# First loads on two queues, a new start order, relu before full-width transposes, and three output tiles side by side, in a fused attention and feed-forward kernel

## The chip, the cores and the metric

The kernel runs on one core of a Trainium2 chip. The metric is the time of one execution on the device in microseconds (us); the kernel before took 325.9 us (median of three runs, 325.85 to 326.36). The granted clock of TensorE was 0.994 to 1.0 of full speed.

## The reference

A linear attention (cosFormer) over 8 batches of 8 heads, 576 positions and head size 64, followed by a gated feed-forward layer over the 4608 tokens:

```python
r   = max(x, 0);  phi(x) = concat(r * cos(theta_s), r * sin(theta_s))   # for q and k, theta_s = pi/2 * s/576
kv  = einsum('bhsf,bhsd->bhfd', phi(k), v)        # 128 x 64 for each head
num = phi(q) @ kv;  den = phi(q) @ sum_s phi(k) + 1e-6
x   = (num / den), heads side by side             # 4608 x 512
g   = x @ w_gate                                  # 512 x 1536
out = (g * sigmoid(g) * (x @ w_val)) @ w_out      # 1536 x 512
```

This is shortened from the reference's code. Per batch and head, `kv` sums phi(k) times v over the positions.

## The kernel before

All matrix work is in bf16. Tokens are handled in nine groups of 512; each group has 12 feed-forward chunks ("chunk 6" is columns 768 to 895 of the gate and value weights) and an output stage of four tiles of 128 tokens. From group two on, a group's attention work is hidden between the products of the group before it. Only at the start is there nothing to hide behind, so the first batch has code of its own. Its inputs are loaded in fp32 by SyncE, in the order in which they are needed; all weights and later inputs are loaded by GpSimd:

```python
load_first("v", slice(0, 2))
load_first("v", slice(2, 4))
load_first("q", slice(0, G), 0, 2)          # q of the first two slots only
load_first("k", slice(0, 2))
load_first("k", slice(2, 4), 0, KCUT)
load_first("k", slice(2, 4), KCUT, NC)
# ... later, GpSimd starts its own loads when a piece of v has landed:
nc.gpsimd.tensor_copy(out=hold, in_=first["v"][:, 1, 0, 0:1])
load_slots(0, "q", QCUT, 4)
# ...
```

ScalarE computes the sines; VectorE then weights v with them, once for each of the four pairs of heads (`vmul`). The order of the first batch's steps on all engines is a list of words. `cq` casts q, `tq` turns (transposes) it, `qr` is its relu, `qw` its weighting, `rk` the relu of k, `kv` the k-v product, `z8` eight products with zeros, put in to keep TensorE busy while it waits, `a` the attention product, `den rec x` the division, `xt xc` the turn of the result, `G V s m` the feed-forward products, silu and multiplication; `@act` and `@dve` choose ScalarE or VectorE:

```python
words = """
    cq0@act cq1@act tq0 qr0@dve qw0.0 qw0.1 rk1.0@act rk0.0@dve z8 kv0.0 rk3.0@dve rk2.0@dve kv1.0
    # ... cut ...
```

q of the second batch is turned by TensorE in the middle of group one (the kernel's group 0). Two transposes of half width, one for each half of a head pair, fill one block of 128 columns; the relu is part of the copy out of the bank:

```python
def qturn_pe(b, j, lo, hi, eng):
    ps = take(1).bitcast(BF16).rearrange("p (c x) -> p c x", x=P)
    for c in range(lo, hi):
        for i in range(2):
            nc.tensor.transpose(out=ps[i * D:(i + 1) * D, c - lo], in_=raws[b, "q"][:, 2 * j + i, c],
                                identity=ident)
    relu_op(eng, qt_of(b)[:, :, j, lo:hi].rearrange("p e c s -> p c e s"), ...)
```

In three places: `turn_last` (four half transposes behind chunk 9), the main turn before the k-v product of batch two (28), and a second turn in the output stage (eight). Chunks 6 to 11 of this group run in two halves of 256 tokens.

## Time and profile before

| What (us from the span's start) | Before |
|---|---|
| Time, median of four runs beside the changed kernel | 325.88 |
| Profiled span | 324.6 |
| TensorE busy | 98% |
| First v lands / first q lands / k's first half lands | 4.4 / 8.0 / 9.5 |
| First k-v product | 11.00 |
| Chunk 6 starts | 28.75 |
| Main turn of batch two's q | 39.66 |
| Group two starts (its first gate product) | 55.48 |

The timeline of the kernel before (columns: start, length, engine, line, operation, shapes, count, and in brackets the idle time before it and what ended that) near its start:

```profile
4.44 1.36 DVE L236 TENSOR_TENSOR v<-wo_sb,tab 128x1152 bf16<-128x1152 f32 x1 [0.41 <-DMA wo_sb<-in_v_dram]
10.29 1.53 DVE L217 TENSOR_SCALAR raw_k<-ht 128x576 bf16<-128x576 f32 x5
11.99 0.74 POOL L203 DMA_DIRECT2D wg_sb<-in_moe_w_gate_dram  x1 [1.40 <-DMA raw_q<-in_q_dram]
```

VectorE waits only 0.41 us for v. Its relus of k fall into a stretch (10.6 to 12.0) in which GpSimd issues nothing. And the timeline of the same kernel in the output stage, around the second turn, with the main turn ahead:

```profile
39.66 0.97 PE L264 MATMUL banks<-ident,raw_q 128*64 128x128 bf16 x28
...
52.22 1.03 PE L539 MATMUL banks<-wo_sb,ht 128*128 128x512 bf16 x4
53.18 0.41 PE L264 MATMUL banks<-ident,raw_q 128*64 128x128 bf16 x8
53.52 1.04 PE L539 MATMUL banks<-wo_sb,ht 128*128 128x512 bf16 x4
```

A length in such a line runs to the modelled end of the last product, so read the distance of starts. Four products of 512 columns take 4 x 0.216 = 0.86 us, but from 52.22 to 53.18 it is 0.96: about 0.1 us passes at the change to half width, and then 0.34 us for the eight transposes.

The landing times come from the DMA issues of the first microseconds (what, queue, count, size, us from issue to landing, the median where there are several); q was issued at 1.75:

```profile
wo_sb<-in_v_dram SPq DMA_DIRECT2D x2, 576.0 KB, 4.1
first_q<-in_q_dram SPq DMA_DIRECT2D x1, 256.0 KB, 6.2
```

(v is loaded into the home of the output weights, hence its name. Its two halves took 3.6 and 4.6 us; issued at 0.74 and 1.27, they landed at about 4.4 and 5.9.)

### The profile page before, as it was taken

What the parts mean: (1) busy time and instruction counts of PE and PEld (TensorE: products, weight loads), DVE (VectorE), ACT (ScalarE), POOL (GpSimd) and SP (SyncE); (2) the same over time, 40 slices, a digit from 0 to 9 for tenths busy, and PEclk for the clock granted to TensorE, in tenths of its full rate; (3) what the DMA queues carried; (4) which work ended last, traced back from release to release, by engine and by line L of the source; (5) the groups of instructions that cost most, each with busy time, mean ns of one, the idle gap of its engine ahead of it and who ended that gap; (6) DMA issues with size and microseconds to landing.
All of it is one profiled execution on the core that took longest, in us unless ns stands there. A gap on an engine that the chain in (4) does not pass through costs nothing.

```text
span 324.6 us, 6212 instructions
## 1 busy us (share of the span) xinstructions
PE 318.0 (98%) x2474; PEld 164.6 (51%) x2474; DVE 181.8 (56%) x366; ACT 132.3 (41%) x247; POOL 34.8 (11%) x58
## 2 busy tenths in 40 slices
PE   7999999999999999999999999999999999999995
PEld 3589855454545444544454445444554445444443
DVE  7775866976575647565657555755564236423420
ACT  7553565943653335332642354344432132213311
POOL 6755200002002000110002000200000000000000
PEclk9999999999999999999999999999999999999999
DMA  7999999499676997699689969794921411240014
GB/s 264 215 199 199 205 205 221 70 125 149 147 125 80 185 153 128 93 170 163 120 111 140 164 129 130 119 186 110 134 46 34 106 26 32 44 103 17 2 32 97
DMA packets 71660, 40.37 MB, mean 124 GB/s; under 512 B 47184, under 2 KB 66384, under 8 KB 71632
## 3 DMA queue, kind: packets, MB, share of 16 engines
q1 hardware_dynamic: 49280, 22.29, 37.9%
q0 software_dynamic: 22192, 17.57, 35.5%
q8 instruction: 19, 0.31, 0.4%
q10 hardware_dynamic: 160, 0.13, 0.1%
q14 instruction: 9, 0.07, 0.1%
HBM read 37.75 MB, written 9.44 MB: 145 GB/s over the span
## 4 chain that ended last, share of the span: by engine, by line
PE 95%; DMA 2%; DVE 1%; ACT 0%; SPq 0%; issue 0%; ACTq 0%
PE banks L503 58%; PE banks L539 28%; PE banks L276 3%; PE banks L390 2%; DMA first_q<-in_q_dram 2%; PE banks L475 1%; PE banks L434 1%; PE banks L149 1%; PE banks L558 1%; PE banks L264 0%; PE banks L316 0%; PE banks L372 0%; SPq L117 0%; DVE qwT L360 0%; ACT ob L561 0%; ACT qf L339 0%
## 5 line engine op out<-in xcount | busy, mean ns | idle before, releaser
L514 DVE TENSOR_TENSOR ht<-sg,banks 128x512 bf16<-128x512 bf16 (+2 forms) x122 | 75.8, 625 | 68.1 <-PE banks L503 62.3
L509 ACT ACTIVATE sg<-banks 128x512 bf16<-128x512 f32 (+2 forms) x122 | 66.9, 548 | 113.6 <-PE banks L503 109.0
L503 PE MATMUL banks<-xT,wv_sb 128*128 128x512 bf16 (+2 forms) x488 | 112.8, 355 | 0.1
L503 PE MATMUL banks<-xT,wg_sb 128*128 128x512 bf16 (+2 forms) x488 | 112.6, 355 | 0.0
L539 PE MATMUL banks<-wo_sb,ht 128*128 128x512 bf16 x420 | 94.3, 379 | 0.0
L503 PEld LDWEIGHTS <-wv_sb 128*128 128x128 bf16 x488 | 47.2, 98 | 46.7 <-issue 0.4
L503 PEld LDWEIGHTS <-wg_sb 128*128 128x128 bf16 x488 | 45.7, 98 | 41.6
L539 PEld LDWEIGHTS <-ht 128*128 128x128 bf16 x420 | 40.1, 98 | 45.2 <-issue 0.2
L546 ACT COPY ob<-banks 128x512 f32<-128x512 f32 x18 | 10.5, 585 | 51.2 <-PE banks L539 49.2
L232 DVE TENSOR_TENSOR r_q<-raw_q,tab 128x1152 bf16<-128x1152 bf16 x24 | 17.9, 754 | 20.2 <-ACT raw_q L215 20.2
L546 DVE COPY ob<-banks 128x512 f32<-128x512 f32 x17 | 11.8, 691 | 28.9 <-PE banks L539 28.0
L236 DVE TENSOR_TENSOR v<-raw_v,tab 128x1152 bf16<-128x1152 bf16 x31 | 23.0, 752 | 0.3 <-ACT raw_v L570 0.3
L411 DVE TENSOR_TENSOR x<-banks,rec 128x512 bf16<-128x512 f32 (+1 forms) x32 | 21.5, 674 | 1.1
L714 POOL COPY hold<-phit 1x2 bf16<-1x2 bf16 x5 | 0.9, 176 | 155.1 <-DMA phit<-r_q 155.1
L215 ACT ACTIVATE raw_q<-raw_q 128x576 bf16<-128x576 bf16 x24 | 15.7, 680 | 0.8 <-DMA raw_q<-in_q_dram 0.8
L215 ACT ACTIVATE raw_k<-raw_k 128x576 bf16<-128x576 bf16 x24 | 16.0, 675 | 0.0
L390 PEld LDWEIGHTS <-phit 128*128 128x128 bf16 (+1 forms) x240 | 9.9, 100 | 6.0 <-issue 1.3
L390 PE MATMUL banks<-kv,phit 128*128 128x65 bf16 (+1 forms) x240 | 11.5, 195 | 0.0
L149 PE MATMUL banks<-zeros 128*128 128x64 bf16 (+1 forms) x66 | 8.7, 290 | 1.0 <-DVE zeros L144 1.0
L299 DVE CAST kv<-banks 64x260 bf16<-64x260 f32 x12 | 5.1, 428 | 7.4 <-ACT kv L299 7.4
L276 PEld LDWEIGHTS <-raw_k 64*64 64x64 bf16 x504 | 7.5, 106 | 2.6 <-issue 2.1
L276 PE MATMUL banks<-v,raw_k 64*64 64x130 bf16 x504 | 8.7, 218 | 0.0
(79 smaller groups left out, 134.3 us busy)
## 6 DMA issues: line engine op xcount, KB each, us to landing
out_dram<-ob SPq DMA_DIRECT2D x70, 128.0 KB, 2.4
raw_k<-in_k_dram POOLq DMA_DIRECT2D x7, 576.0 KB, 9.6
raw_q<-in_q_dram POOLq DMA_DIRECT2D x6, 576.0 KB, 6.1
raw_v<-in_v_dram POOLq DMA_DIRECT2D x6, 576.0 KB, 12.3
wo_sb<-in_moe_w_out_dram POOLq DMA_DIRECT2D x3, 512.0 KB, 12.7
wg_sb<-in_moe_w_gate_dram POOLq DMA_DIRECT2D x5, 256.0 KB, 9.0
wv_sb<-in_moe_w_val_dram POOLq DMA_DIRECT2D x5, 256.0 KB, 9.2
wo_sb<-in_v_dram SPq DMA_DIRECT2D x2, 576.0 KB, 4.1
```

The costliest lines, as they stand in the source:

```text
L149: nc.tensor.matmul(out=ps, lhsT=zeros, rhs=zeros[:, 0:cols].unsqueeze(1).to_broadcast([P, 4, cols]), start=True, stop=True)
L215: nc.scalar.activation(out=out, in_=in_, func=AF.Relu)
L232: nc.vector.tensor_tensor(out=st[b, "q"][:, g], in0=o.unsqueeze(2).to_broadcast([P, NC, 2, D]), in1=tab, op=ALU.mult)
L236: nc.vector.tensor_tensor(out=v2s[b % 2][:, g, :, :, 0:D], in0=(first if b == 0 and g == 0 else {"v": raw_of(b, "v")})["v"][:, g].unsqueez ...
L276: nc.tensor.matmul(out=ps[i * D:(i + 1) * D, e, j * 2 * D1:(j + 1) * 2 * D1], lhsT=raws[b, "k"][es, g, c], rhs=v2s[b % 2][es, g, c, :, 0:D ...
L390: nc.tensor.matmul(out=ps[ms, e, g * D1:(g + 1) * D1], lhsT=phit[b][:, e, g, c:c + n].rearrange("p c s -> p (c s)"), rhs=kv2s[b % 2][:, e, ...
L411: nc.vector.tensor_tensor(out=st["x", t].rearrange("p (y e d) -> p e y d", e=2, d=D)[:, :, ys], in0=ps[:, :, 0:2 * J * D1].rearrange("p e ...
L503: nc.tensor.matmul(out=st["f", tg, fc, lo][i], lhsT=(wg_sb, wv_sb)[i][:, kc, fs], rhs=xT[tg][:, ts, kc], start=(kc == 0), stop=(kc == KC - 1))
L509: nc.scalar.activation(out=sg[:, 0:n], in_=st["f", tg, fc, lo][0], func=AF.Silu)
L514: nc.vector.tensor_tensor(out=hts[tg % 2][:, fc, r:r + n], in0=st.pop(("s", tg, fc, lo))[:, 0:n], in1=ps[1], op=ALU.mult)
L539: nc.tensor.matmul(out=o_ps[t], lhsT=hts[tg % 2][:, fc, r:r + P], rhs=wo_sb[:, fc], start=(fc == 0), stop=(fc == FC - 1))
L546: (nc.scalar.copy if t % 2 == 0 else nc.vector.tensor_copy)(out=ob, in_=ps)
```

## The change

The intent is to shorten the start by issuing the first loads from two engines, to rearrange the start's words for the new landing times, and to save TensorE's small costs in group one. The diff, cut to its core:

```diff
     load_first("v", slice(0, 2))
-    load_first("v", slice(2, 4))
+    load_first("v", slice(2, 4), queue=nc.scalar)
     load_first("q", slice(0, G), 0, 2)
-    load_first("k", slice(0, 2))
+    load_first("k", slice(0, 2), queue=nc.scalar)
     load_first("k", slice(2, 4), 0, KCUT)
-    load_first("k", slice(2, 4), KCUT, NC)
+    load_first("k", slice(2, 4), KCUT, NC, queue=nc.scalar)
 # ... qturn_pe: from the relued copy, full width
-            for i in range(2):
-                nc.tensor.transpose(out=ps[i * D:(i + 1) * D, c - lo], in_=raws[b, "q"][:, 2 * j + i, c],
-                                    identity=ident)
-        relu_op(eng, ...)
+            nc.tensor.transpose(out=ps[:, c - lo], in_=st["qp"][:, b, c, j], identity=ident)
+        copy_op(eng, ...)
 # ... words: the whole list is new; its beginning
-        cq0@act cq1@act tq0 qr0@dve qw0.0 qw0.1 rk1.0@act rk0.0@dve z8 kv0.0 rk3.0@dve rk2.0@dve kv1.0
+        cq1@act cq0@dve tq0 qr0@dve rk0.0@act rk1.0@dve qw0.0 qw0.1 z6 kv0.0 rk2.0@dve rk3.0@dve kv1.0
 # ... batch two's v weightings (vmul) and the new relu between them, on VectorE
-    for g, s in enumerate(("a10", "a11", "b8", "b9")):
+    for g, s in enumerate(("b9", "b9", "b10", "b10")):
         at(s, lambda g=g: vmul(1, g))
+        if g == 2:
+            at(s, lambda: relu_slots(1, 0, CUT))
 # ... chunks 6 to 11 in one piece; three output tiles side by side
-    for nm, f in order:
-        ffn_fc(0, f, *((HALF, GH) if nm == "b" else (0, HALF)))
-        slot(f"{nm}{f}")
+    for f in range(6, FC):
+        ffn_fc(0, f)
+        slot(f"a{f}")
+        slot(f"b{f}")
-    steps0 = [(piece, t) for piece in range(3) for t in range(2)] + [(piece, t) for t in (2, 3) for piece in range(3)]
+    steps0 = [(piece, t) for piece in range(3) for t in range(3)] + [(piece, 3) for piece in range(3)]
```

Cut: the choice of a PSUM bank, pool sizes, the division in two halves, small relus at other slots, and the move of one relu of batch two's k from VectorE to ScalarE.

More of the change, by code (lines that the diff above doesn't have):

```diff
@@ L50 @@
     phip = ctx.enter_context(tc.tile_pool(name="phip", bufs=2))
-    xp = ctx.enter_context(tc.tile_pool(name="xp", bufs=3))
+    xp = ctx.enter_context(tc.tile_pool(name="xp", bufs=4))
     xtp = ctx.enter_context(tc.tile_pool(name="xtp", bufs=3))
     smp = ctx.enter_context(tc.tile_pool(name="smp", bufs=3))
-    sgp = ctx.enter_context(tc.tile_pool(name="sgp", bufs=4))
+    sgp = ctx.enter_context(tc.tile_pool(name="sgp", bufs=5))
     obp = ctx.enter_context(tc.tile_pool(name="obp", bufs=4))
@@ L66, in take @@
     def take(n, hold=None):
-        free = [b for b in range(0, 8, n) if not any(b <= x < b + n for r in held.values() for x in r)]
-        b0 = min(free, key=lambda b: sorted(used[b:b + n], reverse=True))
+        taken = {x for r in held.values() for x in r}
+        free = [b for b in range(0, 8, n) if not any(b <= x < b + n for x in taken)]
+        b0 = min(free, key=lambda b: (n == 1 and hold is not None and hold[0] == "o" and b ^ 1 not in taken,
+                                      sorted(used[b:b + n], reverse=True)))
         if hold is not None:
@@ L114, with load_first @@
         first[nm] = flat.bitcast(FP32).rearrange("p (g c d) -> p g c d", g=G, c=NC)
-    def load_first(nm, gs, lo=0, hi=NC):
-        nc.sync.dma_start(out=first[nm][:, gs, lo:hi].rearrange("p g c d -> p g (c d)"),
+    def load_first(nm, gs, lo=0, hi=NC, queue=nc.sync):
+        queue.dma_start(out=first[nm][:, gs, lo:hi].rearrange("p g c d -> p g (c d)"),
                           in_=source(0, nm)[:, gs, lo * D:hi * D])
@@ L258, in qturn_dma, with relu_slots @@
         )
+    def relu_slots(b, lo, hi):
+        if "qp" not in st:
+            both = rel.tile([P, G, NC, 2, D], BF16, name="r_q").rearrange("p g c w d -> p (g c w d)")
+            st["qp"] = both.rearrange("p (b c j x) -> p b c j x", b=2, c=NC, j=J)
+        relu_op("dve", st["qp"][:, b, lo:hi].rearrange("p c j (i d) -> p c (j i) d", i=2),
+                raws[b, "q"][:, :, lo:hi].rearrange("p g c d -> p c g d"))
     def qturn_pe(b, j, lo, hi, eng):
@@ L262, in qturn_pe @@
         for c in range(lo, hi):
-            for i in range(2):
-                nc.tensor.transpose(out=ps[i * D:(i + 1) * D, c - lo], in_=raws[b, "q"][:, 2 * j + i, c],
-                                    identity=ident)
-        relu_op(eng, qt_of(b)[:, :, j, lo:hi].rearrange("p e c s -> p c e s"),
+            nc.tensor.transpose(out=ps[:, c - lo], in_=st["qp"][:, b, c, j], identity=ident)
+        copy_op(eng, qt_of(b)[:, :, j, lo:hi].rearrange("p e c s -> p c e s"),
                 ps[:, 0:hi - lo].rearrange("p c (e s) -> p c e s", e=2))
@@ L395, in a_tile2, with x_den, x_rec @@
         x_of(t, ps)
-    def x_den(t, ps):
-        den = smp.tile([P, H, 1], FP32, name="den")
+    def x_den(t, ps, ys=slice(0, 4)):
+        if ys.start == 0:
+            st["den", t] = smp.tile([P, H, 1], FP32, name="den")
         nc.vector.tensor_single_scalar(
-            out=den.rearrange("p (e y) o -> p e y o", e=2),
-            in_=ps[:, :, 0:2 * J * D1].rearrange("p e (y x) -> p e y x", x=D1)[:, :, :, D:D1], scalar=1e-6, op=ALU.add)
-        st["den", t] = den
-    def x_rec(t):
-        rec = smp.tile([P, H, 1], FP32, name="rec")
-        nc.vector.reciprocal(out=rec, in_=st.pop(("den", t)))
-        st["rec", t] = rec
-        st["x", t] = xp.tile([P, d_model], BF16, name="x")
+            out=st["den", t].rearrange("p (e y) o -> p e y o", e=2)[:, :, ys],
+            in_=ps[:, :, 0:2 * J * D1].rearrange("p e (y x) -> p e y x", x=D1)[:, :, ys, D:D1], scalar=1e-6, op=ALU.add)
+    def x_rec(t, ps, ys=slice(0, 4)):
+        if ys.start == 0:
+            st["rec", t] = smp.tile([P, H, 1], FP32, name="rec")
+            st["x", t] = xp.tile([P, d_model], BF16, name="x")
+        nc.vector.reciprocal(out=st["rec", t].rearrange("p (e y) o -> p e y o", e=2)[:, :, ys],
+                             in_=st["den", t].rearrange("p (e y) o -> p e y o", e=2)[:, :, ys])
     def x_mul(t, ps, ys=slice(0, 4)):
@@ L418, in x_of @@
         x_den(t, ps)
-        x_rec(t)
+        x_rec(t, ps)
         x_mul(t, ps)
@@ L620 @@
     words = """
-        cq0@act cq1@act tq0 qr0@dve qw0.0 qw0.1 rk1.0@act rk0.0@dve z8 kv0.0 rk3.0@dve rk2.0@dve kv1.0
-        kvo00@act rk3.1@dve kvo01@act rk2.1@dve kv1.1 tq1 kvo10@act kvo11@dve a0.0 qr1@dve a0.1 qw1.0 tq3
-        qw1.1 tq2 den0 qr3@act rec0 x0.0 a1.0 a1.1 qr2@act x0.1 xt0.0 qw3.1 xt0.1 xc0.0@act qw3.0 xc0.1@act
-        den1 z2 a3.0 rec1 G1.0 x1.0 a3.1 s1.0 G0.0 V0.0 qw2.0 s0.0 xt1.0 qw2.1 V1.0 xc1.0@dve a2.0 a2.1 m1.0
-        G1.1 den3 den2 V1.1 rec3 s1.1 G2.01 x3.0 G3.01 s2.01 m1.1 V2.01 rec2 s3.01 x2.0 xt3.0 V3.01
-        xc3.0@act m2.01 xt2.0 m3.01 G5.01 xc2.0@dve G4.01 s5.01 m0.0 G0.23 s4.01 V0.23 s0.23 G1.23 m0.23
-        G5.23 s1.23 V1.23 s5.23 V4.01 m1.23 V5.23 m4.01 V5.01 m5.23 G2.23 m5.01 V2.23 s2.23 G3.23 m2.23
-        V3.23 s3.23 G4.23 m3.23 V4.23 s4.23 G0.1 m4.23 V0.1 s0.1 m0.1
+        cq1@act cq0@dve tq0 qr0@dve rk0.0@act rk1.0@dve qw0.0 qw0.1 z6 kv0.0 rk2.0@dve rk3.0@dve kv1.0
+        kvo01@act rk3.1@dve kvo00@act rk2.1@dve kv1.1 a0.0 kvo11@act kvo10@dve tq1 den0.0 rec0.0 a0.1 x0.0
+        qr1@act tq2 den0.1 rec0.1 qw1.1 tq3 qr2@act qw1.0 xt0.0 x0.1 a1.0 qr3@act a1.1 qw2.0 xt0.1 qw2.1
+        xc0.0@act den1 z2 a2.0 rec1 xc0.1@act a2.1 x1.0 G1.0 G0.0 qw3.1 s1.0 xt1.0 s0.0 qw3.0 V0.0 xc1.0@act
+        V1.0 den2 rec2 a3.0 x2.0 a3.1 G0.1 G1.1 den3 s0.1 V1.1 rec3 s1.1 xt2.0 x3.0 G2.01 xc2.0@act V0.1
+        m1.0 V2.01 s2.01 m0.0 m0.1 xt3.0 m1.1 G3.01 m2.01 xc3.0@act V3.01 s3.01 G1.23 m3.01 V1.23 s1.23
+        G0.23 m1.23 V0.23 s0.23 G5.23 m0.23 G4.01 s5.23 G2.23 s4.01 G4.23 s2.23 G5.01 s4.23 V5.01 s5.01
+        V5.23 m5.01 G3.23 m5.23 V3.23 s3.23 V4.23 m3.23 V2.23 m4.23 V4.01 m2.23 m4.01
     """.split()
@@ L634 @@
         whole, a, part = b not in ("0", "1") or a != "0", int(a), int(b or 0)
+        ys = slice(0, 4) if whole else slice(2 * part, 2 * part + 2)
         if op == "z":
@@ L653 @@
         elif op == "den":
-            x_den(a, st["a", a])
+            x_den(a, st["a", a], ys)
         elif op == "rec":
-            x_rec(a)
+            x_rec(a, st["a", a], ys)
         elif op == "x":
-            x_mul(a, st["a", a], slice(0, 4) if whole else slice(2 * part, 2 * part + 2))
+            x_mul(a, st["a", a], ys)
             st["a", a, "n"] = st.get(("a", a, "n"), 0) + 1
@@ L674 @@
                 ffn_mul(0, a, *span)
-    order = []
-    for f in range(6, FC, 2):
-        order += [("a", g) for g in (f, f + 1)]
-        order += [("b", g) for g in (f, f + 1)]
     def turn_last():
@@ L684, in turn_last @@
             qturn_pe(0, j, NC - 1, NC, "act")
+    at("a8", lambda: relu_slots(0, NC - 1, NC))
     at("b9", turn_last)
     at("a8", lambda: relu_k(1, 0, 2, "dve"))
-    at("a9", lambda: relu_k(1, 2, 4, "dve"))
-    for g, s in enumerate(("a10", "a11", "b8", "b9")):
+    at("a9", lambda: relu_k(1, 2, 4, "act"))
+    for g, s in enumerate(("b9", "b9", "b10", "b10")):
         at(s, lambda g=g: vmul(1, g))
+        if g == 2:
+            at(s, lambda: relu_slots(1, 0, CUT))
     at("b11", q_(1, 0, 0), q_(1, 1, 0), lambda: kv_mm(1), lambda: kv_out(1))
@@ L699 @@
     at((2, 0), turn(6, True))
+    at((0, 3), lambda: relu_slots(1, CUT, NC))
     at((2, 1), q_(1, 0, 1), q_(1, 1, 1))
     at((2, 2), turn(7, True))
-    HALF = GH // 2
-    for nm, f in order:
-        ffn_fc(0, f, *((HALF, GH) if nm == "b" else (0, HALF)))
-        slot(f"{nm}{f}")
-    steps0 = [(piece, t) for piece in range(3) for t in range(2)] + [(piece, t) for t in (2, 3) for piece in range(3)]
+    for f in range(6, FC):
[3 more added lines that the diff above has]
+    steps0 = [(piece, t) for piece in range(3) for t in range(3)] + [(piece, 3) for piece in range(3)]
     for i, (piece, t) in enumerate(steps0):
```

## The prediction

> **What bounds the kernel now.** I read the page's busy shares and slices first, then the chain that ended last in order of time, then the groups by shape, the start of the timeline, and the landing of each early transfer.
>
> ```profile
> PE 318.0 (98%) x2474; PEld 164.6 (51%) x2474; DVE 181.8 (56%) x366; ACT 132.3 (41%) x247; POOL 34.8 (11%) x58
> PEclk9999999999999999999999999999999999999999
> L503 PE MATMUL banks<-xT,wv_sb 128*128 128x512 bf16 (+2 forms) x488 | 112.8, 355 | 0.1
> L503 PE MATMUL banks<-xT,wg_sb 128*128 128x512 bf16 (+2 forms) x488 | 112.6, 355 | 0.0
> L539 PE MATMUL banks<-wo_sb,ht 128*128 128x512 bf16 x420 | 94.3, 379 | 0.0
> ```
>
> TensorE is at full clock in every slice and has almost no idle time before its feed-forward products: it is the bound. But a busy TensorE also counts products with zeros, so I look at the chain for time in which it does no useful work.
>
> ```profile
> 1.75 6.24 DMA first_q<-in_q_dram
> 8.01 0.72 ACT qf L339 x2
> 8.78 0.34 PE banks L347 x3
> 9.12 1.73 PE banks L149 x8
> ...
> 12.78 0.43 DVE kvd L324
> 13.21 0.34 DVE qr L217
> 13.58 0.76 DVE qwT L360 x2
> 14.34 0.09 DVE den L399
> ...
> 15.78 0.43 PE banks L149 x2
> ...
> 23.94 11.96 PE banks L503 x112
> 35.90 0.23 PE banks L264 x4
> 36.13 3.60 PE banks L503 x32
> 39.73 0.90 PE banks L264 x28
> 40.63 1.17 PE banks L276 x67
> 41.81 0.97 PE banks L539 x4
> ```
>
> The columns are start, length, what. Useful work starts at 8.5 us, when the first q has landed and been cast. Then come 1.73 us of zero products (L149) that wait for k, and a VectorE stretch from 12.78. Counting every useful product at its streaming time (512 columns: 10.36/48 = 0.216 us; 256: 11.96/112 = 0.107; 128 and 130: 0.055) I get about 306 us; the last matmul ends at 319.8, so 13.6 us are bubbles: 8.5 before the first useful product, about 4.1 from there to 24 us, about 1 after. From the start of token group two's up products (55.5 us) the changed program's TensorE instructions are the same as before, so the change is worth exactly what it moves that point.
>
> **What the Trainium skill says.** (1) "DMA: Bandwidth & Descriptors", Issuing engines are not separate DMA queues: transfers from any engine run on the same 16 DMA engines and interleave; a second issuer saves only sequencer time. The trace agrees as far as it can: with one queue the engines are full from about 2.3 us. The DMA view of the first 45 us, in 40 slices:
>
> ```profile
> DMA  0489999999999999999999999999999999999999
> GB/s 0 72 317 410 343 310 380 349 246 200 182 178 183 201 193 195 197 195 205 193 207 210 198 194 190 191 192 202 217 200 203 202 210 210 206 205 207 208 214 187
> ```
>
> (2) "Perfetto Trace Analysis", DMA Instruction - HWDGE: the issuing sequencer is free for its next instruction only when descriptors are generated. The tail of the timeline agrees: a copy queued behind a ScalarE issue starts after it.
>
> ```profile
> 320.26 0.56 ACTq L564 DMA_DIRECT2D out_dram<-ob  x1
> 320.94 0.32 ACT L561 COPY ob<-banks 128x192 f32<-128x192 f32 x1 [0.71 <-PE banks L558]
> ```
>
> (3) "TensorE: Matmul & The Clock Gate", Back-to-back issue gap: the spacing at full clock grows with the columns (262 cycles for 256, 518 for 512). The trace agrees (107 and 216 ns), so splitting a 512-wide product in two costs almost nothing, and joining it gains almost nothing. (4) Same page, Packing small matmuls: products on different parts of the array run together. The trace agrees: 28 half-width transposes took 0.90 us, 32 ns each, where four full ones take 0.22 us, 55 ns each.
>
> **The change part by part.**
>
> *Two queues.* ScalarE now issues three loads before its table load. At 0.5 to 0.56 us each that is some 1.6 us: its table load would start at 2.3 instead of 0.74, and the sine table be done some 1.0 us later (before, it idled 0.58 us waiting for the angles). VectorE's tab, then its four weightings of v, follow the sine; in the trace the latter end at 4.44 + 1.36 and 6.06 + 2.10 = 8.16, so now near 9.2. The cast of half of q stands behind them on VectorE. Against that, k's first half no longer queues behind q. It landed at 2.27 + 7.2 = 9.5 us; at the measured 350 to 400 GB/s, v (1.18 MB) lands by 5.3 and q and that half of k (0.85 MB, less the share of the GpSimd loads) by about 8. So the 1.73 us wait for k disappears, but the wait for q becomes a wait for VectorE. Estimated: q cast by 9.45, turned by 9.85, relu of q and of k 10.9, first k-v product at 11.0, which is when it starts now. The extra landing time of k is thus spent by the later start of ScalarE, if the issues cost what they cost at the tail; if they hide, all of this is 1 us earlier.
>
> *New order of words.* Before, q's second relu and two weightings (0.34 + 0.76) stood between the k-v copy and the first denominator. They move behind it: 1.1 us off the path to the first x half. But the second half of x now stands behind two weightings, and the token tile that is turned first waits for both. Following the order by hand with these durations, the first gate product comes at about 17.2 (before 16.4), with 0.2 us more of useful work already done and some 0.2 us fewer bubbles after. Net: about 0.3 us late under the full ScalarE delay, 0.7 us early without it.
>
> *Feed-forward chunks 6 to 11 at full width.* Before, twelve half chunks (eight 256-wide products each) took 0.876 us apiece, 10.5 us; 48 products of 0.216 give 10.36. Gain 0.15 us. VectorE and ScalarE save more: twelve evictions of 418 ns become six of 687, off the path.
>
> *Full transposes.* 40 half ones took 0.23 + 0.90 + 0.34 = 1.47 us; 20 full ones at 0.055 take 1.1. Gain 0.37 us. But the relu now comes before the turn, on VectorE, and not in the copy after it. With X the start of chunk 6: VectorE does the chunk-9 product until X + 7.7, two v weightings (1.5), the chunk-10 product (0.69), a third weighting (0.75), then this relu of 1792 elements (estimated 0.7 from 0.45 to 0.65 us for 1152): X + 11.4. TensorE is through with chunk 11 at X + 10.5. It would wait 0.9 us, unless VectorE runs ahead of this count.
>
> *Three output tiles side by side.* Same products. Output weights are needed one to two steps later, which makes room to start earlier (the first third lands near 40.3 and is used at 41.7). No gain by itself.
>
> Sum at the 55.5 us point: +0.3 (or -0.7) -0.15 -0.37 +0.9 (or about 0.3 if the VectorE queue is less full than I count) = +0.7 in the worst reading, -0.9 in the best. The middle is -0.1. The new order has plainly been fitted to the new landing times, so that I lean to the better half and take -0.5: 325.4 us.
>
> **The rivals.** (a) *The start is moved later by ScalarE.* The tail's 0.56 us speaks for it, and the idle 0.58 us before the sine hides only a part. It makes 326 to 326.8. (b) *The weights become the bound.* If the start is 2 us earlier, TensorE meets transfers: chunk 1's value weights land at 8.33 + 7.7 = 16.0 us, batch two's q at 27.16 + 10.6 = 37.8, and through relu (0.7), turns (0.8) and k-v product (1.2) this allows output products no earlier than 40.5, against 41.7 now. So about 1.3 us is the most that the start can give, whatever it does: 324.2 with the rest. Against it: it matters only if all before goes well. (c) *q lands later* because its 512-byte pieces share each DMA engine with k's 2304-byte ones. It took 2.6 us after v for 256 KB even alone on its queue. If it lands at 9.3, the result is that of (a). (d) *PSUM:* three open output tiles leave four banks for the second batch's products; a bank waiting for VectorE's combination (about 1 us for each half) would add 0.2 to 0.5 us.
>
> **Range and chances.** The best case is bounded by the transfers (about -1.5 us), the worst is (a) with the stall at the relu and (d) (about +1.2 us). Low 324.0, high 326.8, centre 325.4. Two percent is 6.5 us, which is more than all bubbles after 8.5 us, and nothing here adds as much: faster by over 2% 0.01, within 2% 0.98, slower by over 2% 0.01.
>
> **What would show it.** Right: k's first half lands over 1 us earlier, no run of six or eight zero products waits for k, ScalarE's sine near 3.6 us, VectorE's weightings of v ending near 9.2, first k-v product near 11.0; a gap of 0.5 to 0.9 us on TensorE before the full transposes, ended by VectorE; the rest shifted as one. Wrong: the first k-v product at 10 or earlier (issues on ScalarE cost nothing), or no wait before the transposes; then the time falls toward 324. Idle TensorE in front of weight loads ended by a DMA would show rival (b), before the second batch's products ended by VectorE rival (d). A time outside the range needs a stall that repeats in each later group, which the unchanged order of instructions there speaks against.

## The result, and the profile after

The changed kernel took 327.95 us (median of four runs, 327.2 to 329.06) against 325.88 (325.66 to 326.36) for the kernel before on the same chip: ratio 1.0063, 95% interval 1.004 to 1.0087. That is within 2%, but slower, and above the predicted range. All outputs are right. A ratio here is always the mean time of one kernel's runs over the mean of the other's in the same rounds, so not quite the ratio of the medians.

The profile's page still says that TensorE is the bound:

```profile
PE 317.8 (97%) x2404; PEld 160.4 (49%) x2404; DVE 182.3 (56%) x362; ACT 133.4 (41%) x244; POOL 34.8 (11%) x58
```

The span went from 324.6 to 326.3. Group two starts at 57.22 instead of 55.48, 1.74 us later, and the last TensorE work ends at 321.52 instead of 319.78, again 1.74. So everything was lost before group two. The chain of the changed kernel (start, length, what):

```profile
1.27 8.10 DMA first_q<-in_q_dram
9.39 0.63 DVE qf L348
...
10.51 0.42 DVE qr L220
10.93 0.73 DVE raw_k L220
...
12.32 1.41 DVE raw_k L220 x4
...
40.59 1.00 DVE r_q L220
41.64 0.96 PE banks L274 x14
```

Before, the chain went through q's landing at 7.99 and was on TensorE from 23.94 on. Now q lands at 9.37, VectorE stands in the chain with its cast and its relus of k, and it comes back at 40.59 with the new relu. The DMA issues of the first microseconds show why the start is late; SyncE issued q at 1.27:

```profile
wo_sb<-in_v_dram SPq DMA_DIRECT2D x1, 576.0 KB, 5.1
wo_sb<-in_v_dram ACTq DMA_DIRECT2D x1, 576.0 KB, 5.5
first_q<-in_q_dram SPq DMA_DIRECT2D x1, 256.0 KB, 8.1
```

q is issued 0.48 us earlier than before and takes 1.9 us longer. The two halves of v no longer land one after the other (4.4 and 5.9) but almost together (5.8 and 6.2): the first half, all that the first weighting needs, now takes 5.1 us instead of 3.6. The timeline lines that answer to those shown of before:

```profile
2.36 1.28 ACT L177 ACT_TABLE_LOAD   x1 [2.36 <-issue]
5.96 1.36 DVE L239 TENSOR_TENSOR v<-wo_sb,tab 128x1152 bf16<-128x1152 f32 x1 [0.88 <-DMA wo_sb<-in_v_dram]
12.25 1.48 DVE L220 TENSOR_SCALAR raw_k<-ht 128x320 bf16<-128x320 f32 x4
12.05 0.82 POOL L206 DMA_DIRECT2D wg_sb<-in_moe_w_gate_dram  x1
...
41.64 0.96 PE L274 MATMUL banks<-ident,r_q 128*128 128x128 bf16 x14 [0.89 <-DVE r_q L220]
```

ScalarE's three issues delay its table load from 0.74 to 2.36. The first v weighting moved from 4.44 to 5.96, still waiting for the load. The main turn waits 0.89 us for VectorE. And in the output stage full transposes fit without a seam:

```profile
54.18 1.03 PE L549 MATMUL banks<-wo_sb,ht 128*128 128x512 bf16 x4
55.05 0.39 PE L274 MATMUL banks<-ident,r_q 128*128 128x128 bf16 x4
55.27 1.03 PE L549 MATMUL banks<-wo_sb,ht 128*128 128x512 bf16 x4
```

0.87 and 0.22 us, where the half transposes needed 0.96 and 0.34.

The balance by distances of starts, in the two traces:

| Step | Before | After | Difference |
|---|---|---|---|
| Chunk 6 starts | 28.75 | 30.12 | +1.37 |
| Chunks 6 to 11 and `turn_last`, to the end of the last product | 10.82 | 10.48 | -0.34 |
| From there to the main turn | 0.09 | 1.04 | +0.95 |
| Main turn, k-v product | 2.08 | 2.06 | -0.02 |
| Output stage | 13.74 | 13.52 | -0.22 |
| Sum: start of group two | 55.48 | 57.22 | +1.74 |

(The last product before the turn starts, as one of four, in a row at 39.13 before and 39.73 after; adding four times 0.109 or 0.216 gives 39.57 and 40.60. The profile's 0.89 us counts from the modelled end of that product, which is 0.15 later. The changed kernel's trace is of an execution of 328.08 us, 0.9 above its fastest, and that of the kernel before of one of 326.36, the slowest of its four. So 1.74 is the difference of these two executions; the medians differ by 2.07 here and by 1.28 in the repetition e5.)

### The profile page after: what moved, and what is told of

It reads as the page before. It is cut to its first block, busy times and chain, and to the rows that moved or that the text cites. A ratio compares the mean times of both kernels' runs of the same rounds, so it can differ in the third digit from the quotient of the medians.

```text
span 326.3 us, 6058 instructions
## 1 busy us (share of the span) xinstructions
PE 317.8 (97%) x2404; PEld 160.4 (49%) x2404; DVE 182.3 (56%) x362; ACT 133.4 (41%) x244; POOL 34.8 (11%) x58
## 4 chain that ended last, share of the span: by engine, by line
PE 93%; DVE 3%; DMA 2%; ACT 0%; issue 0%; ACTq 0%; SPq 0%
PE banks L513 56%; PE banks L549 28%; PE banks L285 3%; DMA first_q<-in_q_dram 2%; PE banks L399 2%; PE banks L485 1%; PE banks L444 1%; PE banks L381 1%; DVE raw_k L220 1%; DVE v L239 1%; PE banks L568 1%; DVE ht L524 0%; DVE qwT L369 0%; PE banks L274 0%; DVE r_q L220 0%; ACT ob L571 0%
## 5 line engine op out<-in xcount | busy, mean ns | idle before, releaser
L524 DVE TENSOR_TENSOR ht<-sg,banks 128x512 bf16<-128x512 bf16 (+2 forms) x116 | 74.8, 650 | 69.3 <-PE banks L513 63.8
L519 ACT ACTIVATE sg<-banks 128x512 bf16<-128x512 f32 (+2 forms) x116 | 65.8, 568 | 111.9 <-PE banks L513 108.1
L513 PE MATMUL banks<-xT,wv_sb 128*128 128x512 bf16 (+2 forms) x464 | 111.3, 364 | 0.0
L513 PE MATMUL banks<-xT,wg_sb 128*128 128x512 bf16 (+2 forms) x464 | 111.2, 364 | 0.0
L513 PEld LDWEIGHTS <-wv_sb 128*128 128x128 bf16 x464 | 44.9, 98 | 48.7
L513 PEld LDWEIGHTS <-wg_sb 128*128 128x128 bf16 x464 | 43.4, 98 | 43.3
L218 ACT ACTIVATE raw_k<-raw_k 128x576 bf16<-128x576 bf16 (+1 forms) x25 | 17.2, 695 | 0.0
```

Of the source, the lines that this page charges most:

```text
L218: nc.scalar.activation(out=out, in_=in_, func=AF.Relu)
L513: nc.tensor.matmul(out=st["f", tg, fc, lo][i], lhsT=(wg_sb, wv_sb)[i][:, kc, fs], rhs=xT[tg][:, ts, kc], start=(kc == 0), stop=(kc == KC - 1))
L519: nc.scalar.activation(out=sg[:, 0:n], in_=st["f", tg, fc, lo][0], func=AF.Silu)
L524: nc.vector.tensor_tensor(out=hts[tg % 2][:, fc, r:r + n], in0=st.pop(("s", tg, fc, lo))[:, 0:n], in1=ps[1], op=ALU.mult)
```

## The experiments

Theory at the outset: the second queue delays the first products, and the relu ahead of the turn adds a stall; the other parts save a little. Rivals: ScalarE's issuing alone is to blame; the new words are; or the runs differ by chance. Twelve kernels were run. All times are us, the first five columns from each kernel's trace, the last two from timed runs.

| Run | q's cast on ScalarE | First k-v product | Chunk 6 | Main turn (wait as the profile counts it) | Group two | Median | Ratio to before, 95% interval |
|---|---|---|---|---|---|---|---|
| before | 8.01 | 11.00 | 28.75 | 39.66 (0) | 55.48 | 325.88 | 1 |
| changed | 9.39 | 11.92 | 30.12 | 41.64 (0.89) | 57.22 | 327.95 | 1.0063, 1.004 to 1.0087 |
| e1 | 7.26 | 10.42 | 28.09 | 39.61 (0.89) | 55.19 | 326.19 | 1.0009, 0.9995 to 1.0023 |
| e2 | 9.09 | 12.26 | 30.24 | 41.15 (0) | 56.97 | 327.86 | 1.0059, 1.0046 to 1.0071 |
| e3 | 9.20 | 11.45 | 29.29 | 40.15 (0.22) | 55.72 | 326.63 | 1.0030, 1.0016 to 1.0045 |
| e4 | 7.94 | 11.00 | 28.75 | 39.66 (0) | 55.48 | 326.16 | 1.0007, 0.9995 to 1.0020 |
| e5 | 9.12 | 11.67 | 29.88 | 41.40 (0.89) | 56.97 | 327.21 | 1.0049, 1.0032 to 1.0065 |
| e6 | 7.75 | 10.53 | 28.21 | 39.00 (0) | 54.94 | 325.64 | 0.9991, 0.9978 to 1.0004 |
| e7 | 7.95 | 11.24 | 29.11 | 40.63 (0.89) | 56.21 | 326.91 | 1.0028, 1.0016 to 1.0040 |
| e8 | 7.51 | 11.34 | 29.28 | 40.80 (0.89) | 56.38 | 327.25 | 1.0040, 1.0028 to 1.0052 |
| e11 | 7.15 | 9.76 | 27.70 | 38.49 (0) | 54.43 | 325.30 | 0.9981, 0.9969 to 0.9993 |
| e12 | 7.58 | 10.57 | 28.31 | 39.10 (0) | 54.92 | 325.82 | 0.9996, 0.9982 to 1.0010 |

(e9 and e10 are not in the table, as they have waits of their own.) A trace is one execution, and the start jitters: with one queue q landed between about 6.9 and 8.0 us, with two between about 9.05 and 9.37, in different runs. A difference of some tenths in one trace proves nothing; I rely on intervals of timed runs, and on traces for where the time is. The medians of "before" in the five sets of rounds were 325.88 to 326.03.

### e1: the changed kernel with all first loads on SyncE

```diff
-    load_first("v", slice(2, 4), queue=nc.scalar)
+    load_first("v", slice(2, 4))
-    load_first("k", slice(0, 2), queue=nc.scalar)
+    load_first("k", slice(0, 2))
-    load_first("k", slice(2, 4), KCUT, NC, queue=nc.scalar)
+    load_first("k", slice(2, 4), KCUT, NC)
```

> The changed kernel with all six first loads back on SyncE, nothing else. Theory (queues are the first cause): q shared each DMA engine with the first half of k and landed at 9.37 instead of 7.99 us, v at 5.9 instead of 4.4; on one queue q lands near 8.0 again, the first k-v product comes near 10.2 (k lands near 9.5) instead of 11.92, and the time falls by 1.3 to 2 us, to about 326.2. Rival (the new word order is what is slow): the start gains under 0.5 us although q lands early.

Measured: 326.19 us, ratio 1.0009; the interval includes 1. Taking the second queue away gives back 1.75 us by the medians with the first runs of the changed kernel (327.95), 1.3 us by ratio with its repetition e5 (1.0049 less 1.0009). The four relus of k are fast again, and GpSimd pauses beside them (from 10.63 to 11.21):

```profile
10.75 0.95 DVE L220 TENSOR_SCALAR raw_k<-ht 128x320 bf16<-128x320 f32 x4
```

The stall before the turn stays at 0.89. So it does not come from the start.

### e2: the kernel before with the loads alternating

```diff
-    load_first("v", slice(2, 4))
+    load_first("v", slice(2, 4), queue=nc.scalar)
-    load_first("k", slice(0, 2))
+    load_first("k", slice(0, 2), queue=nc.scalar)
-    load_first("k", slice(2, 4), KCUT, NC)
+    load_first("k", slice(2, 4), KCUT, NC, queue=nc.scalar)
```

> The kernel before with only the queues alternated. Theory: q lands near 9.4, and because the old order puts both k relus behind q's weightings the start is late by 1 to 1.5 us: 326.9 to 327.4. Rival (queues are harmless, k's earlier landing pays for q's later one): within 0.3 us of 325.9.

Measured: 327.86 us, ratio 1.0059, above the 326.9 to 327.4 expected. Two queues alone, with the old words and the old turns, cost 1.9 us: as much as the whole change. q is cast at 9.09, 1.08 later than before, and TensorE's turn waits for it:

```profile
9.09 0.71 ACT L339 CAST qf<-first_q 128x256 bf16<-128x256 f32 x2 [0.86 <-DMA first_q<-in_q_dram]
```

The five relus of k took 2.34 us together instead of 1.53. Chunk 6 starts 21.15 us after the cast of q here, 20.73 to 20.83 in before, changed, e1 and e5. In these traces, then, the new words take back about 0.4 us of what two queues cost the old ones; in e3's, which has the same start as the changed kernel, it is 1.1 (20.09). With one queue they lie between 0.1 us later (e1) and 0.3 sooner (e6, 20.46). These are single traces.

### e3: the relu of batch two before the third v weighting

```diff
     for g, s in enumerate(("b9", "b9", "b10", "b10")):
-        at(s, lambda g=g: vmul(1, g))
         if g == 2:
             at(s, lambda: relu_slots(1, 0, CUT))
+        at(s, lambda g=g: vmul(1, g))
```

> The changed kernel with the relu of batch two's q put before the third v weighting on VectorE instead of behind it. Theory (the 0.9 us wait of TensorE before the full transposes is VectorE's queue): the wait shrinks by one weighting, 0.7 us, to some 0.2 us, and the time by 0.6 to 0.7 us, to about 327.3. Rival (the wait is for q's transfer, which landed at 37.9 us, or is caught up later in any case): under 0.2 us.

Measured: 326.63 us, ratio 1.0030, below the 327.3 expected. The wait shrank by 0.67 us to 0.22, as the place of one weighting (0.75, of which 0.67 from start to start) in VectorE's order says:

```profile
40.15 0.96 PE L274 MATMUL banks<-ident,r_q 128*128 128x128 bf16 x14 [0.22 <-DVE r_q L220]
```

The median fell by 0.58 against e5; ratios 1.0030 and 1.0049 agree with that. This trace also reached chunk 6 0.6 to 0.8 us sooner than the changed kernel's two, because VectorE's cast of q took 0.29 instead of 0.63 us and its first relu of k 0.45 instead of 0.82. As nothing of the start was edited, that is jitter; the section on e9 shows what it goes with. The five times of e3 fall into two groups (326.55 to 326.63, and 327.35 and 327.42), and its trace is from the lower one, while those of the changed kernel and of e5 are from executions 0.9 and 0.7 above their fastest. The lesson of the run is the stall alone.

### e4: the kernel before with three small loads ahead on ScalarE

```diff
+    small = [consts.tile([P, 16], FP32, name=f"small_{i}") for i in range(3)]
+    for i in range(3):
+        nc.scalar.dma_start(out=small[i], in_=source(0, "v")[:, i, 0:16])
     load_first("v", slice(0, 2))
```

> The kernel before with three loads of 8 KB more, issued by ScalarE at the same place as in the change: the cost of issuing without the sharing. If ScalarE's lost 1.6 us are the cause, the sine ends near 3.9 us, v's weightings near 9.2 and the time rises by 1 us or more; if the sharing of the DMA engines is the cause, q still lands near 8.0, the relu of q is at most 0.3 us later, and the wait for k at 9.5 to 10.9 swallows most: under 0.4 us, about 326.2.

Measured: 326.16 us, ratio 1.0007: nothing to tell from zero. The issues did delay the sines by about 0.9 us (table load at 2.16), but in the old order both casts of q and the first relu of k are on ScalarE and VectorE's queue has slack there; the first k-v product stayed at 11.00. In this trace q landed early (7.15) and its cast still started only at 7.94, so the delay was there, hidden under the usual landing time of q.

### e7: the same three small loads in the new order, with one queue

The edit is that of e4, made to e1.

> The changed kernel on one queue, with three 8 KB loads more issued by ScalarE at the place of the change: the issue cost in the new word order, where a cast of q stands behind v's weightings on VectorE. Prediction's step (ScalarE's issues make the sine 1 us late, v's weightings end near 9.2 and the first k-v product 0.7 to 1 us later than on one queue): 326.8 to 327.2 us. Rival (sharing alone is the cost): within 0.3 us of 326.2.

Measured: 326.91 us, ratio 1.0028, and 0.72 us above e1 by the medians (0.6 by the ratios). In the new order, half of q is cast by VectorE, behind its weightings of v, which wait for the sines. Those weightings now end at 9.02, and the first k-v product moves from 10.42 to 11.24:

```profile
2.17 1.28 ACT L180 ACT_TABLE_LOAD   x1 [2.17 <-issue]
...
6.93 2.09 DVE L242 TENSOR_TENSOR v<-raw_v,tab 128x1152 bf16<-128x1152 bf16 x3 [0.85 <-ACT raw_v L583]
```

The same three issues cost nothing in one order and 0.7 us in the other.

### e8: only the second half of v on ScalarE

```diff
-    load_first("k", slice(0, 2), queue=nc.scalar)
+    load_first("k", slice(0, 2))
-    load_first("k", slice(2, 4), KCUT, NC, queue=nc.scalar)
+    load_first("k", slice(2, 4), KCUT, NC)
```

> The changed kernel with only the second v load on ScalarE; q and all of k stay behind the first v load on SyncE. Theory (loads in flight together share the engines, each then lands late): both v land late, at 5.5 to 5.9 us, but q, which no k shares with, lands by 8.3; VectorE's weightings still end near 9.3, so that the start stays late by 1 us: 327.0 or more. Rival (only q's landing counts): the first k-v product near 10.7 and 326.3 us.

Measured: 327.25 us, ratio 1.0040, as slow as the repeated change. Here the sines are on time and q, issued at 1.27 as in the change, lands at 7.07: so it is k's load beside it that makes q late by some 2 us in the change. But both halves of v land near 5.8, and that is enough:

```profile
5.87 1.36 DVE L239 TENSOR_TENSOR v<-wo_sb,tab 128x1152 bf16<-128x1152 f32 x1 [1.83 <-DMA wo_sb<-in_v_dram]
```

The weightings end at 9.23, where they end in the change (9.32, and 9.21 in e5). So late v, late q and ScalarE's issues lie side by side: late v alone, with what hangs on it (GpSimd's loads start when v lands), makes most of the loss (e8), the issues alone 0.7 us (e7), late q was not tried alone. Taking one away leaves the others, and their costs must not be added.

### e5: the changed kernel once more

> The changed kernel once more, unchanged, so that this chip and these rounds have their own number for it. 327.2 to 328.1 us; TensorE waits 0.9 us before the full transposes; q lands between 9.0 and 9.4 us.

The edit is one empty line at the end of the file. Measured: 327.21 us (327.13 to 328.96), ratio 1.0049, interval 1.0032 to 1.0065. The result repeats: slower than before by 0.3 to 0.9%. The size is uncertain by about half a microsecond, as single executions of this kernel scatter upwards (its two highest are 327.81, the one traced, and 328.96).

### e6: one queue, and the relu back in the copy

The edit is that of e1, and in addition the turn as before:

```diff
-            nc.tensor.transpose(out=ps[:, c - lo], in_=st["qp"][:, b, c, j], identity=ident)
-        copy_op(eng, ...)
+            for i in range(2):
+                nc.tensor.transpose(out=ps[i * D:(i + 1) * D, c - lo], in_=raws[b, "q"][:, 2 * j + i, c],
+                                    identity=ident)
+        relu_op(eng, ...)
-    at("a8", lambda: relu_slots(0, NC - 1, NC))
-        if g == 2:
-            at(s, lambda: relu_slots(1, 0, CUT))
-    at((0, 3), lambda: relu_slots(1, CUT, NC))
```

> The changed kernel with one queue, and with batch two's q turned as before: half-width transposes straight from the loaded tile, the relu in the copy behind them. Theory (the two causes add: queues about 1.75 us, relu ahead of the turn about 0.9): the wait before the transposes is gone and, as 28 half transposes took 0.90 us against 0.96 for 14 full ones, nothing is lost: about 325.3 us, which would beat both kernels. Rival (the wait only moves to a transfer, q of batch two landing near 37.8): no faster than 326.0.

Measured: 325.64 us, ratio 0.9991; 325.3 was expected. No wait is left before the turn:

```profile
39.00 0.97 PE L275 MATMUL banks<-ident,raw_q 128*64 128x128 bf16 x28
```

Against e1 this is 0.55 us faster by the medians, although it gives up the full transposes. From chunk 6 to group two it takes 26.73 us, e1 27.10. e1 without its extra wait (1.04 by starts, less the 0.09 that half transposes need there) would take 26.15. But e6 has a small wait of its own: its first output product starts 0.16 us later after the turn than in the kernel before (2.24 against 2.08), and the chain of its first 60 us runs from v's landing at 4.46 through GpSimd's issues to the load of the output weights, which lands at 41.20:

```profile
29.60 11.60 DMA wo_sb<-in_moe_w_out_dram
```

Without it 26.57 would be left. The full transposes are thus worth about 0.4 us here, and the relu ahead of them costs about 1. The small wait is what the prediction's rival (b) describes, weights that come too late for an earlier start; e11 shows it too (2.24).

### e9 and e10: GpSimd's loads started later

These ask whether GpSimd's loads and issues beside the start are the hidden cause. e9 is e1 with GpSimd's hold on a later piece of v; e10 is e6 with the hold on q, and with the casts and first relus of k on ScalarE.

```diff
 # e9
-    nc.gpsimd.tensor_copy(out=hold, in_=first["v"][:, 1, 0, 0:1])
+    nc.gpsimd.tensor_copy(out=hold, in_=first["v"][:, 3, 0, 0:1])
 # e10
-    nc.gpsimd.tensor_copy(out=hold, in_=first["v"][:, 1, 0, 0:1])
+    nc.gpsimd.tensor_copy(out=hold, in_=first["q"][:, 0, 0, 0:1])
-        cq1@act cq0@dve tq0 qr0@dve rk0.0@act rk1.0@dve ...
+        cq1@act cq0@act tq0 qr0@dve rk0.0@act rk1.0@act ...
```

> The changed kernel on one queue, but GpSimd's first issues wait for the second v load instead of the first, about 1 us later, so that they fall on VectorE's relus of k. Theory (VectorE's relus of fp32 k slow down while GpSimd writes its issues: four took 0.95 us where GpSimd was idle and 1.48 where it was busy): the four take some 1.4 us, q lands earlier, and the time is 0.1 to 0.5 us above the 326.2 of one queue. Rival (the slow relus come from the two queues themselves): the four stay at 0.95 us and the time at or below 326.2.

> A candidate: one queue, relu in the copy behind the turn, GpSimd's first issues held until q has landed (the opposite of sharing: q and k have the DMA engines to themselves), both casts of q and both relus of k's first half on ScalarE. Theory: q lands near 6.8 us, k's first half near 8, the first k-v product near 9.5 instead of 10.5, and the time about 325.0; it can gain at most 1.2 us at batch two's q, which lands near 37.8 whatever comes first. Rival (weights then come late and the first gate product waits for them): no faster than 325.6.

Measured: e9 326.63 us, ratio 1.0027 (1.0014 to 1.0040). The four relus of k, now beside GpSimd's issues, are as slow as in the change though there is one queue:

```profile
10.43 1.52 DVE L220 TENSOR_SCALAR raw_k<-ht 128x320 bf16<-128x320 f32 x4
```

They took 0.95 where GpSimd paused (e1, e6), and 1.47 to 1.52 in every trace in which it issued throughout (changed, e3, e5, e8, e9). That association is shown; how much of the total it makes is not, because e9 also made later transfers late: TensorE waited 0.8 us for q's next slots and 2.0 us for the relu before the turn, which itself waited 1.05 us for batch two's q. Moreover its trace is of its slowest execution (327.73; the other five took 326.59 to 326.70).

The start times show more. A relu that begins 0.27 us after GpSimd began to issue (first two lines, the changed kernel) is long; one that begins 0.23 us after it (last two, e9) is not, and there the issue is long:

```profile
10.58 0.80 POOL L206 DMA_DIRECT2D wg_sb<-in_moe_w_gate_dram  x1
10.85 0.82 DVE L220 TENSOR_SCALAR raw_k<-ht 128x576 bf16<-128x576 f32 x1
...
9.16 0.99 POOL L207 DMA_DIRECT2D wv_sb<-in_moe_w_val_dram  x1
9.39 0.45 DVE L220 TENSOR_SCALAR raw_k<-ht 128x576 bf16<-128x576 f32 x1
```

I counted all 76 relus of the first k and casts of the first q on VectorE in the fourteen traces. The 41 that begin outside a GpSimd issue, or at most 0.24 us into one, take 0.27 to 0.32 us (0.45 for 576 elements). The 35 that begin 0.25 us or more into one end 0.09 to 0.15 us after that issue ends (0.28 to 0.29 for 576 elements), and so take up to 0.83. There is no exception. So what looked like jitter of VectorE goes with where its work falls in GpSimd's row of issues, and that row starts with the landing of v.

e10: 326.88 us, ratio 1.0038 (1.0017 to 1.0060). A miss: q landed at 7.85, no sooner than with GpSimd's transfers under way (6.85 to 7.99 with one queue), so this trace gives no sign that those delay it; TensorE then waited 1.0 us for the next slots of q and 0.4 us for output weights. Against e11, which differs by the hold alone, that is 1.6 us: in this kernel GpSimd's loads must not be held back that long.

### e11: e6 with both casts of q and both first relus of k on ScalarE

```diff
-        cq1@act cq0@dve tq0 qr0@dve rk0.0@act rk1.0@dve qw0.0 qw0.1 z6 kv0.0 ...
+        cq1@act cq0@act tq0 qr0@dve rk0.0@act rk1.0@act qw0.0 qw0.1 z6 kv0.0 ...
```

> The same without the hold: one queue, relu in the copy, both casts of q and both relus of k's first half on ScalarE. It tells the part of the hold from the part of the engines. Theory: k lands near 9.3, two relus in a row on ScalarE end near 10.6, so the first k-v product stays near 10.6 and the time at 325.5 to 325.8.

Measured: 325.30 us (324.95 to 325.69), ratio 0.9981, interval 0.9969 to 0.9993: faster than both kernels, if only by 0.2%, and better than the 325.5 to 325.8 expected. That it beats e6 is not shown (the intervals overlap). The first k-v product was expected near 10.6 with k at 9.3; in this trace k's first half landed at 8.8 and the product starts at 9.76, since q's cast and the second relu no longer stand behind VectorE's weightings:

```profile
8.79 1.26 ACT L218 ACTIVATE raw_k<-ht 128x576 bf16<-128x576 f32 x2 [0.93 <-DMA ht<-in_k_dram]
```

In e1 the second of these relus was VectorE's and ended at 10.16; here ScalarE has done both by 10.05 and VectorE is free for the weightings of q.

### e12: the kernel before with full-width chunks and three output tiles only

```diff
-    for nm, f in order:
-        ffn_fc(0, f, *((HALF, GH) if nm == "b" else (0, HALF)))
-        slot(f"{nm}{f}")
+    for f in range(6, FC):
+        ffn_fc(0, f)
+        slot(f"a{f}")
+        slot(f"b{f}")
-    steps0 = [... two tiles at a time ...]
+    steps0 = [... three tiles side by side ...]
-    for g, s in enumerate(("a10", "a11", "b8", "b9")):
+    for g, s in enumerate(("b9", "b9", "b10", "b10")):
```

The choice of banks and one pool's size are also taken from the change.

> The kernel before (one queue, its own order of words, half transposes, relu in the copy) with only the last two of the change's parts: chunks 6 to 11 at full width, and three output tiles side by side, for which batch two's v weightings move to the change's slots. Theory (these parts give a little, 0.15 to 0.4 us, between chunk 6 and token group two, as the traces of the change show): about 325.6, with chunk 6 to the turn about 10.7 us instead of 10.9 and no wait before the turn. Rival (they give nothing, or the open banks stall TensorE): 325.9 or more, with a wait of TensorE on a copy out of the banks in the output stage.

Measured: 325.82 us, ratio 0.9996 (0.9982 to 1.0010): by the time alone theory and rival can't be told apart. The trace can: from chunk 6 to the main turn (39.10) 10.79 us instead of 10.91, and no wait on open banks. From the main turn to group two it is 15.82 us in both. So full-width chunks give 0.12 us and three tiles side by side nothing. The rest of the trace's earlier end is q's earlier landing (7.58 against 8.01 to its cast).

## Why the prediction was wrong, point by point

**The bound and what decides: right.** TensorE stayed the bound, and group two's shift of 1.74 us appears unchanged at TensorE's last end. No two-percent change was possible, and the class "within 2%" came true.

**Two queues: the mechanism was seen, the size was not.** ScalarE's issue time (1.6 us) and the later sines (3.65) were right. The end of the v weightings (9.32, "near 9.2") came out right partly by luck: in the trace the first weighting waited 0.88 us for v, not for the sines, and either delay alone gives that end (9.02 in e7, 9.23 in e8). Wrong is the estimate "v (1.18 MB) lands by 5.3 and q and that half of k ... by about 8": v's second half landed at 6.2 and q at 9.37. In the trace before the change v's second half had landed only at 5.9, which the median that the prediction read (4.1 us for two issues of 3.6 and 4.6) hides; for the same reason q came 2.1 us after v there, not 2.6. The working treated the loads as a sum of bytes at one rate. k did gain (9.5 to 8.3), but its bytes came out of q's share, and q is needed first. The first k-v product came at 11.92 instead of 11.0 (11.67 in e5). The prediction had this as rival (c), with 9.3 as the landing time, and put its result at that of rival (a), 326 to 326.8; both were undersized. Not foreseen at all was that the relus of k fall beside GpSimd's issues, whose start hangs on v's landing, and take 1.48 us instead of 0.95 (e1).

**New words: right as an order, wrong as a sum.** Predicted net 0.3 us late for the start in the worst reading; chunk 6 was 1.37 us late. This is the term of the sum that failed most. But it was not the words: measured from q's cast, they bring chunk 6 at least 0.4 us sooner than the old words do with two queues (20.73 against 21.15 in e2). With the new words and ScalarE's issues but without the sharing (e7), chunk 6 was 0.36 us late, as predicted. What made it later is the landing of v and q: v's weightings ended at 9.32 and q landed at 9.37, so that either alone would have held up the start, and with q early again (e8) nothing was gained.

**Full-width chunks: right.** Predicted 0.15, e12 shows 0.12 (one trace).

**Full transposes: right in sum, for a different reason.** Predicted 0.37 saved. Measured by starts: 0.23 around `turn_last` (chunk 6 to the end of the last product 10.71 in e12, 10.48 after), 0.09 and 0.01 at the main turn, 0.22 in the output stage, about 0.55 in all. (e6 against e1 gives about 0.4, with the 0.09 left out.) The prediction multiplied counts by 55 and 32 ns. In the main turn this alone saves almost nothing (14 full ones took 0.89 us to the next product's start, 28 half ones 0.90). What it missed is the pause of about 0.1 us at each change of width, which the short turns no longer pay. The Trainium skill states it, "TensorEngine Tiling (Array Packing)", Key Properties: changing the tiling mode drains TensorE. The prediction had not looked there.

**Relu before the turn: right.** Predicted a wait of 0.9 us; the profile shows 0.89, in the changed kernel and in four of the five others that kept its order on VectorE (e1, e5, e7, e8; in e9, where batch two's q landed late, 2.0). The exact hit is partly luck: TensorE was through at X + 10.48 as counted (X is the start of chunk 6), but the relu took 1.08 us, not 0.7, and the four operations between the chunk-9 product and the relu took 2.52 us, not 2.94. e3 and e6 confirm the cause.

**Three output tiles: right.** No gain (e12), and rival (d), a stall on PSUM, did not occur.

**Rival (b)** (weights as the bound) did not occur: no wait of TensorE for a weight load in the changed kernel. It did, by 0.16 us, where the start was made faster (e6, e11).

**The step that failed** is the landing times under *Two queues* ("v (1.18 MB) lands by 5.3 and q and that half of k ... by about 8"), and with them the start's term of the sum: +0.3 at the worst, measured +1.37 (+1.13 in e5's trace). v's halves landed at 5.8 and 6.2 and q at 9.37; one queue again (e1) gave back 1.3 to 1.75 us. The last step made it worse: "The new order has plainly been fitted to the new landing times, so that I lean to the better half and take -0.5". The worked sum in the worst reading was +0.7; rivals (a) and (c) came true together; the stall of 0.9 had a count behind it and was talked down. The stated high end, 326.8, also lies below the prediction's own worst case (325.9 + 1.2 = 327.1). With the measured start term (+1.37 instead of +0.3) and full transposes as they are, the same sum gives +1.37 - 0.12 - 0.55 + 1.04 = +1.74. The trust in the tuning had no row of the profile under it. By the trace of e2 the new order does fit two queues better than the old one did, by 0.4 us or more, and this is far from paying for them.

What stays open: why VectorE's work is long beside a GpSimd issue that is under way (no run isolates it), and how the loss at the start splits between late v, late q and slow relus, since each hides behind the others. A version that would keep the full transposes with an early relu (e3) in the order of e11 was not run.

## What to carry to other kernels

When the DMA engines are already full, a second issuing queue does not make the first loads faster as a whole: here it took bytes from the loads that are needed first (v, q) and gave them to those needed later (k), so keep what is needed first alone at the head. Before moving an operation out of a copy and ahead of TensorE (here the relu), count the queue of the engine that inherits it, and believe that count. When several delays run side by side, test each alone as well as all together: here the late v made most of the loss by itself, and giving q its early landing back saved next to nothing.

## What the Trainium skill lacked or had wrong

- "DMA: Bandwidth & Descriptors", Issuing engines are not separate DMA queues: agrees that transfers interleave, but speaks only of saved sequencer time. It has no figure for what sharing costs the load that is needed first: with the second half of v on another queue both halves landed near 5.8 us, where the first was there at 4.4 before (e8); with k beside it q landed 1.4 us later (9.37 against 7.99).
- "DMA: Bandwidth & Descriptors", SWDGE vs HWDGE vs iDMA: speaks of GpSimd being locked out by VectorE (that it can be the other way round stands elsewhere in the skill). No page says from which moment of an issue VectorE is the one that waits: here work that began 0.25 us or more into an issue ended 0.09 to 0.29 us after it, and work that began up to 0.24 us into it was not lengthened.
- "TensorEngine Tiling (Array Packing)", Key Properties: says that a mode change drains TensorE, without a figure. Here about 0.1 us passed at each change from 128x128 to 128x64.
- "TensorE: Matmul & The Clock Gate", Back-to-back issue gap: gives a sustained 131 ns for 512 columns and 81 ns for 128; the traces show 216 ns, and 55 ns for four transposes in a row (0.22 us), so the formula that the page calls isolated is the one that fits here. The page's own measured gaps in other sections (215.7 and 55.6 ns) agree with it.
- No page says how far the landing of a first load varies from run to run; q's landing varied by about 1 us with one queue (6.85 in e11, 7.99 before).
